# Partial sums loaded 42 products ahead, maxima turned before a run of products, stores listed two steps later

## The chip, the cores and the metric

The kernel runs on one core of a Trainium2 chip. The metric is the time of one execution on the device, in microseconds. Of several executions the median is given. The profile is one further execution, recorded by the hardware profiler; its own time is in the table below. In its lines PE is TensorE, DVE is VectorE, ACT is ScalarE, POOL is GpSimd and SP is SyncE, which here only issues transfers.

## What is computed

The input x has 2048 positions of 512 features. Two mixing layers run on it, and a gate for each position mixes their outputs:

```python
def _A_ref(x, dft_seq_re, dft_seq_im, dft_hid_re, dft_hid_im):
    a = jnp.einsum("bsd,ed->bse", x, dft_hid_re)
    b = jnp.einsum("bsd,ed->bse", x, dft_hid_im)
    return (jnp.einsum("ts,bse->bte", dft_seq_re, a)
            - jnp.einsum("ts,bse->bte", dft_seq_im, b))

def _B_ref(x, wqkv, wo):
    # 32 heads of 16 features; position i sees positions i-255 .. i
    ...
    scores = jnp.einsum("bhqd,bhkd->bhqk", q, k) * (Dh ** -0.5)
    p = _softmax(jnp.where(mask, scores, -1e9), axis=-1)
    o = jnp.einsum("bhqk,bhkd->bhqd", p, v)
    return o_as_rows @ wo

g = _sigmoid((x * gate_w).sum(-1, keepdims=True))
return g * _A_ref(...) + (1 - g) * _B_ref(...)
```

Everything is float32. The dense products are made from pairs of float32r tiles, a high part and a low part of each operand, as three products: high by high, high by low and low by high.

## The kernel before

**Two streams on one engine.** PE runs two streams of work, woven into one order written out by hand.

The *dense stream* is the generator `dense()`. It makes q, k and v, the DFT along the features (`ab_part`), and the DFT along the sequence, whose matrices come from HBM in pieces (`Pieces`: `load` brings a raw piece of 512 KB into one of two buffers, `split` makes its high and low parts with ACT at L141 and DVE at L142). Most of it runs in `halves64`: each step issues one product for partitions 0 to 63 (`first`) and one for partitions 64 to 127 (`second`, `DELAY` = 6 steps later). The unit is a `Part`, 12 or 24 products into one PSUM tile of 512 columns, and `second` takes the parts of a group in another order than `first`. An `Out` is the tile that one part, or several, add up in; when its last product has been issued, its `end` is called, which has the tile read out.

The sequence DFT is cut so that many outputs are finished in several rounds, since not all of its inputs fit into SBUF. `store_r` writes a first partial sum (ACT, L746) to a scratch tensor `r_scr` in HBM. A later round loads it again into an SBUF tile of the pool `ev` (five buffers that rotate), and `add_to` (DVE, L757) adds the new PSUM tile to it and stores the result. The load is `Out.load`, made by `fetch`; `product` calls it at L498, at the first product of the output's last half-part. There are 21 such outputs. After the attention `c_block` goes on with whole products (L547) and has its own load.

The *attention stream* runs over 128 blocks, n = 0 to 127: 8 groups of 4 heads by 16 blocks of 128 queries. Each iteration n has four quarters q. In the even ones `s_pair` makes scores of two heads (L338), and DVE masks them and takes their row extremes (L342). In the odd ones, nine iterations behind (`LAG`), `t_pair` makes the same scores transposed with the maxima subtracted (L397), ACT takes the exponential (L400), and POOL cuts the window's edges (L402, L406). Each takes one of two PSUM tiles of the pool `ps_a` in turn; a tile is free again when DVE, or ACT, has read it. `pv` multiplies by v (L420) every fourth iteration.

Every four iterations the maxima go from columns to rows: `ml_split` (DVE, L350 and L351) makes high and low parts, `ml_turn` (PE, L358) transposes them into a tile of `ps_a`, `ml_rows` (ACT, L363) copies them out, `m_out` and `m_ring` bring them through HBM into `ring`, where `t_pair` reads them nine iterations later.

**What sets the order.** The engines work in the order in which the program lists their instructions. In each quarter the loop at L1090 lists `s_pair` or `t_pair`, then what `agenda` holds for time 4n+q, then `fill`, which lists three or four steps of the dense stream (six to eight products), then what `agenda` holds for 4n+q+0.5. So an agenda time that ends in .5 comes behind the run of dense products and a whole one ahead of it. `after(n, fn)` lists a call n steps of the dense stream later. All loads and stores but a few go through SP (`ld`, L65), in the order listed; SP stops at one that has to wait.

**Names that matter here.** `STORE` (8) is the number of steps between the read-out of a PSUM tile into an `ev` tile and the listing of its store: for v (L307), first sums (L747), later sums (L758) and the outputs of `c_block` (L816). `ring_next` (L1024) lists the four loads of a group's next q and k into `ring`, at t+0.5, t+1.5, t+2.5 and t+3.5; t is set at L1080. The offsets of the maxima's steps are at L1066, counted from the third quarter of the last of four iterations.

Of the kernel before, what the change touches and what calls it, by code (L numbers as in the profile page):

```python
# [21 lines left out]
NB = S // P  # L22
# [7 lines left out]
DELAY = 6  # L30
# [4 lines left out]
RING_LATE = 5  # L35
JOB = 4
FIRST_OUT, PAIR = 104, 38
STORE, STORE_HL = 8, 11
FILL_T = 0.75


# [1 line left out]
def fnet_window_mix(ctx: ExitStack, tc: tile.TileContext, xT, x, wqk, wv, wr, wi, cr, ci, wo, gw, out):  # L43
# [84 lines left out]
    def beat():  # L128
        beats[0] += 1
        flush(beats[0])  # L130
# [14 lines left out]
    def job(n):  # L145
        if n % JOB == 0 and jobs:
            jobs.pop(0)()
# [341 lines left out]
    def product(part, half, i):  # L489
        o = part.out  # L490
        if o.ps is None:
            o.ps = ps_d.tile([P, 512], F32, name="d", tag="d")
            start = True
        else:
            start = False
        if part.ops is None:
            part.ops = part.make()
        if i == 0 and o.load and o.left == 1:  # L498
            o.r = o.load()
        lhs, rhs = part.ops[i]  # L500
        end = i == len(part.ops) - 1
        o.left -= end
        r = slice(64 * half, 64 * half + 64)
        nc.tensor.matmul(o.ps, lhs[r], rhs[r], start=start, stop=end and o.left == 0, skip_group_check=True)  # L504
        if end:
            if o.left:
                nc.scalar.copy(tick, o.ps[:, 0:1])
            else:
                o.end(o)

    def halves64(groups):
        first = [(p, i) for g in groups for p in g for i in range(p.n)]
        second = [(p, i) for g in groups for p in [g[-1], *g[:-1]] for i in range(p.n)]
        steps.append(len(first) + DELAY)
        for t in range(len(first) + DELAY):
            taken[0] += 1
            if t < len(first):
                part, i = first[t]
                if i == 0 and part.pre:
                    part.pre()  # L520
                if i in part.mid:
                    part.mid[i]()
                product(part, 0, i)
            if t >= DELAY:
                part_b, i_b = second[t - DELAY]
                product(part_b, 1, i_b)
            if t < len(first):
                job(i + 1)
            beat()
            yield  # L530
# [71 lines left out]
    def dense():  # L602
# [203 lines left out]

        c_groups[0][0].mid[12] = to_c
        yield from halves64(groups + c_groups)
        have.add("halves")

# [241 lines left out]
    def at_time(t, fn, *args):  # L1052
        agenda.setdefault(t, []).append((fn, args))
# [9 lines left out]
        at_time(4 * n + 8, v_spread, i)  # L1063
    for u in range(N // 4):
        t = 4 * (4 * u + 3) + 3
        for d, fn in ((0, ml_split), (2.5, ml_turn), (3, ml_rows), (3, m_out), (8, m_ring)):  # L1066
            at_time(t + d, fn, u)
    for i in range(4 * GROUPS):
        t = 4 * (VISIT * i + VISIT + LAG) + 3
# [7 lines left out]
    at_time(4 * (N + LAG - 12), wo_fetch, 0)  # L1077
    for G in range(1, GROUPS):
        for ss in range(4):
            t = 4 * (NB * G + 4 * ss) - 11.5  # L1080
            at_time(t, ring_next, t, G, ss)

    def run(t):
# [66 lines left out]
```

## Time and profile before

| | |
|---|---|
| median of 3 runs | 873.34 us (871.14 to 874.76) |
| profiled execution, its time | 869.23 us |
| profiled execution, its span | 867.5 us |
| granted TensorE clock, mean | 0.984 |
| DVE busy | 524.8 us (60%) |
| ACT busy | 409.4 us (47%) |
| data moved | 179.29 MB, mean 207 GB/s |

The span runs from the first instruction to the last; the time of the execution holds some 1.7 us more around it. Busy time counts an engine's instructions, and of the transfers the share of 16 DMA engines. A line such as "A <- B: 12.2, 5, 4.7" says that A's engine sat idle for 12.2 us in total, 5 times, at most 4.7 us, and that B ended it. In the timeline the columns are start, duration, engine, line, operation, what it writes and reads, and in brackets the idle time before it. "PEld" is the loading of weights, which lies beside the products.

### The profile page before, as it was taken

The numbers are of one execution on the slowest core, as the hardware profiler recorded it, in microseconds if no ns is written. First come the engines' busy times: TensorE is split into PE (matmuls) and PEld (weight loads), VectorE is DVE, ScalarE is ACT, GpSimd is POOL, SyncE is SP. The second block draws the span as 40 slices with busy tenths as digits, with TensorE's granted clock in tenths as the row PEclk, the third lists the DMA queues.
The fourth block names the chain that finished last, engine by engine and source line by source line (L and its number), as shares of the span: only waits on it lengthen the run. The fifth ranks groups of instructions, "written<-read, shape, count | busy, mean of one in ns | idle before, by whom it ended". The sixth has DMA issues, their size and how long they took to land.

```text
span 867.5 us, 19719 instructions
## 1 busy us (share of the span) xinstructions
PE 829.7 (96%) x7298; PEld 659.4 (76%) x7298; DVE 524.8 (60%) x1504; ACT 409.4 (47%) x794; POOL 315.4 (36%) x590
## 2 busy tenths in 40 slices
PE   8999999999989999999999999879889999899998
PEld 7898777777677777787778777657666778788887
DVE  6376676667566776666467666546556527455442
ACT  6235554556445555555555654335335655231320
POOL 4002333344233333333333343223223445574530
PEclk9999999999999999999999999989999999999999
DMA  8786787787968455545555657777886567765631
GB/s 310 248 257 188 255 263 231 233 259 255 299 231 282 127 169 177 169 142 159 178 159 170 182 183 199 228 222 215 243 255 210 172 194 224 229 217 168 209 109 49
DMA packets 111648, 179.29 MB, mean 207 GB/s; under 512 B 34240, under 2 KB 43968, under 8 KB 111552
## 3 DMA queue, kind: packets, MB, share of 16 engines
q1 hardware_dynamic: 109584, 176.85, 65.1%
q10 hardware_dynamic: 1968, 1.18, 0.5%
q8 instruction: 57, 0.93, 0.5%
q14 instruction: 39, 0.32, 0.1%
HBM read 112.98 MB, written 64.75 MB: 205 GB/s over the span
## 4 chain that ended last, share of the span: by engine, by line
PE 74%; DMA 14%; DVE 6%; issue 2%; SPq 2%; ACT 2%; POOL 1%; DVEq 0%; ACTq 0%; POOLq 0%
PE d L504 40%; PE o L420 8%; PE dc L547 8%; PE s L338 5%; PE t L975 5%; DMA raw<-ci 4%; PE t L397 4%; DVE junk L342 3%; PE d L534 3%; DMA qk_scr<-home 2%; SPq L65 2%; DMA raw<-cr 1%; DMA lt<-ots 1%; DMA ev<-l_scr 1%; DMA ring<-qk_scr 1%
## 5 line engine op out<-in xcount | busy, mean ns | idle before, releaser
L342 DVE CUSTOM_DVE_ANT_0 junk<-s,mask 128x384 f32<-128x384 f32 (+2 forms) x512 | 272.2, 532 | 199.2 <-PE s L338 188.6
L504 PE MATMUL d<-big,hi 64*128 64x512 f32 x1920 | 348.1, 398 | 0.0
L402 POOL TENSOR_SCALAR_AFFINE_SELECT pt<-pt 128x256 f32<-128x256 f32 x256 | 114.6, 447 | 458.8 <-ACT pt L400 357.6
L400 ACT ACTIVATE pt<-t 128x768 f32<-128x768 f32 (+2 forms) x256 | 197.7, 772 | 136.6 <-PE t L397 129.9
L504 PEld LDWEIGHTS d<-big,hi 64*128 64x128 f32 x1920 | 197.7, 189 | 27.3 <-issue 0.6
L504 PE MATMUL d<-big,lo 64*128 64x512 f32 x960 | 207.7, 399 | 0.0
L504 PE MATMUL d<-hi,big 64*128 64x512 f32 x672 | 132.1, 392 | 0.0
L338 PE MATMUL s<-ring,ring 48*128 48x384 f32 (+2 forms) x512 | 98.8, 358 | 20.3 <-DVE ml L342 14.6
L504 PEld LDWEIGHTS d<-big,lo 64*128 64x128 f32 x960 | 101.1, 189 | 13.7 <-issue 0.4
L141 ACT CAST hi<-raw 128x512 fp32r<-128x512 f32 x142 | 87.2, 618 | 35.5 <-DMA raw<-ci 17.3
L397 PE MATMUL t<-ring,ring 50*128 50x384 f32 (+2 forms) x512 | 88.7, 334 | 5.2 <-ACT mhl L363 4.1
L547 PE MATMUL dc<-big,hi 128*128 128x512 f32 x284 | 92.2, 394 | 0.0
L406 POOL TENSOR_SCALAR_AFFINE_SELECT pt<-pt 128x256 f32<-128x256 f32 x224 | 91.4, 408 | 0.0
L142 DVE TENSOR_TENSOR lo<-raw,hi 128x512 fp32r<-128x512 f32 x110 | 82.5, 750 | 13.8 <-ACT hi L141 13.7
L338 PEld LDWEIGHTS s<-ring,ring 48*128 48x128 f32 x512 | 53.6, 186 | 43.6 <-DVE ml L342 20.2
L420 PE MATMUL o<-pt,vt 128*32 128x384 f32 (+2 forms) x1408 | 85.3, 390 | 0.1
L504 PEld LDWEIGHTS d<-hi,big 64*128 64x128 f32 x672 | 75.6, 186 | 7.8
L504 PE MATMUL d<-lo,big 64*128 64x512 f32 x336 | 79.5, 392 | 0.0
L420 PEld LDWEIGHTS o<-pt,vt 128*32 128x32 f32 x1408 | 41.9, 111 | 47.5 <-issue 30.6
L397 PEld LDWEIGHTS t<-ring,ring 50*128 50x128 f32 x512 | 50.7, 187 | 19.7 <-ACT mhl L363 5.6
L547 PEld LDWEIGHTS dc<-big,hi 128*128 128x128 f32 x284 | 52.1, 189 | 8.6 <-DVE mask L871 0.2
L142 POOL TENSOR_TENSOR lo<-raw,hi 128x512 fp32r<-128x512 f32 x32 | 42.5, 1339 | 38.7 <-ACT hi L141 34.6
(113 smaller groups left out, 790.2 us busy)
## 6 DMA issues: line engine op xcount, KB each, us to landing
ring<-qk_scr SPq DMA_DIRECT2D x128, 192.0 KB
qk_scr<-home SPq DMA_DIRECT2D x32, 512.0 KB
raw<-cr SPq DMA_DIRECT2D x32, 512.0 KB
raw<-ci SPq DMA_DIRECT2D x32, 512.0 KB
r_scr<-ev SPq DMA_DIRECT2D x44, 256.0 KB
ab_scr<-home SPq DMA_DIRECT2D x20, 512.0 KB
big<-ab_scr SPq DMA_DIRECT2D x20, 512.0 KB
qk_scr<-home SPq DMA_DIRECT2D x32, 256.0 KB
```

The lines of the kernel that those rows point to most:

```text
L141: jobs.append(lambda c=c: nc.scalar.copy(hi[:, c], raw[:, c]))
L142: jobs.append(lambda c=c: (nc.gpsimd if FIN else nc.vector).tensor_sub(lo[:, c], raw[:, c], f(hi[:, c])))
L338: nc.tensor.matmul(ps[:, h, :w], ring[0][r, p, j * P:j * P + P], ring[1][r, p, k0:k0 + w], start=True, stop=True)
L342: mark("dve", nc.vector.tensor_tensor_reduce(out=junk[:, :w], in0=ps[:, h, :w], in1=mask[:, WIN - w:], scale=1.0, scalar=3e38, op0=OP.add, ...
L397: nc.tensor.matmul(ps[:, h, :w], ring[1][r, p, q0:q0 + P], ring[0][r, p, q0:q0 + w], start=True, stop=True)
L400: nc.scalar.activation(pt[:, ph, :w], ps[:, :, :w], AF.Exp, scale=-1.0)
L402: nc.gpsimd.affine_select(a, a, pattern=[[0, 2], [1, P]], compare_op=OP.is_ge, fill=0.0, base=0, channel_multiplier=-1)
L406: nc.gpsimd.affine_select(a, a, pattern=[[0, 2], [-1, P]], compare_op=OP.is_gt, fill=0.0, base=0, channel_multiplier=1)
L420: nc.tensor.matmul(o[32 * j:32 * j + 32, (a - 4 * c) * P:(e - 4 * c) * P], v[:, kb % 4, 32 * j:32 * j + 32], PT[G * NB + kb][:, j, (a - kb ...
L504: nc.tensor.matmul(o.ps, lhs[r], rhs[r], start=start, stop=end and o.left == 0, skip_group_check=True)
L547: nc.tensor.matmul(ps, w[a][:, i % 8 * 128:i % 8 * 128 + 128], ab[SC[i]][:, b], start=i == ends[0] and a + b == 0, stop=i == ends[1] and a ...
L975: nc.tensor.matmul(ps, o[:, a, c], fin(n, b, c), start=start and c == 0 and a + b == 0, stop=c == 1 and a == 1, skip_group_check=True)
```

## The change

Four numbers or places are changed.

- The load of a partial sum is no longer called in `product`. `halves64` works out for each output that has a load the step of its last product, in either half, and calls the load at the step `FETCH` = 42 before it.
- `STORE` is 10, not 8.
- `ml_turn` has the offset 2, not 2.5: it is listed right behind `t_pair` of the second quarter, ahead of that quarter's dense products, where it was behind them and right ahead of the next `s_pair`.
- The times of `ring_next` start 11 quarters ahead, not 11.5, so that its loads are listed behind a quarter's dense products, not ahead of them.

```diff
-STORE, STORE_HL = 8, 11
+STORE, STORE_HL = 10, 11
+FETCH = 42
...
-        if i == 0 and o.load and o.left == 1:
-            o.r = o.load()
...
+        ends = {}
+        for d, order in ((0, first), (DELAY, second)):
+            for t, (part, _) in enumerate(order):
+                if part.out.load:
+                    ends[part.out] = max(t + d, ends.get(part.out, 0))
+        fetches = {}
+        for o, t in ends.items():
+            fetches.setdefault(t - FETCH, []).append(o)
         for t in range(len(first) + DELAY):
             taken[0] += 1
+            for o in fetches.get(t, ()):
+                o.r = o.load()
...
-        for d, fn in ((0, ml_split), (2.5, ml_turn), (3, ml_rows), (3, m_out), (8, m_ring)):
+        for d, fn in ((0, ml_split), (2, ml_turn), (3, ml_rows), (3, m_out), (8, m_ring)):
...
-            t = 4 * (NB * G + 4 * ss) - 11.5
+            t = 4 * (NB * G + 4 * ss) - 11
```

## The prediction

> **What bounds the kernel now.** I read the page first, then the busy time by stretches.
>
> ```profile
> span 867.5 us, 19719 instructions
> ...
> PE 829.7 (96%) x7298; PEld 659.4 (76%) x7298; DVE 524.8 (60%) x1504; ACT 409.4 (47%) x794; POOL 315.4 (36%) x590
> ```
>
> TensorE (PE) is the bound. The view by windows (stretch, its length, busy time with instructions of PE, PEld, DVE, ACT, POOL, then granted clock, DMA share, GB/s) says where it isn't:
>
> ```profile
> 531.00:534.00 3.00, 3.00 (x32) 2.49 (x30) 2.74 (x8) 2.06 (x3) 0.76 (x2) 1.00 0.66 181
> 567.00:570.00 3.00, 3.00 (x30) 2.40 (x28) 1.28 (x5) 1.98 (x4) 0.85 (x3) 1.00 1.06 287
> 530.00:690.00 160.00, 141.87 (x1332) 107.33 (x1334) 95.20 (x280) 69.84 (x127) 50.30 (x111) 0.95 0.73 221
> 350.00:400.00 50.00, 50.00 (x520) 39.58 (x519) 32.31 (x99) 27.10 (x53) 19.33 (x41) 1.00 0.55 160
> ```
>
> From 350 to 400 us PE has no idle time: whatever makes it wait there adds to the total. From 530 to 690 it idles 18.1 us, with a clock of 0.95. The waits inside that stretch (us in total, times, longest):
>
> ```profile
> PE s L338 <- DVE ml L342: 12.2, 5, 4.7
> ...
> DVE ev L757 <- issue: 7.7, 2, 4.6
> ...
> DVE ev L757 <- DMA ev<-r_scr: 6.3, 2, 4.7
> ...
> DVE ev L757 <- PE t L397: 5.7, 2, 3.8
> ...
> ACT hi L141 <- DMA raw<-ci: 3.3, 2, 2.3
> ...
> PE t L397 <- ACT mhl L363: 1.6, 1, 1.6
> ```
>
> L757 is the add of a partial sum. It sat idle 19.7 us in these six waits. The timeline shows one of them whole:
>
> ```profile
> 562.45 0.58 SPq L65 DMA_DIRECT2D ev<-r_scr  x1
> ...
> 564.26 0.79 SPq L65 DMA_DIRECT2D raw<-ci  x1
> ...
> 573.02 0.75 DVE L757 SCALAR_TENSOR_TENSOR ev<-d,g,ev 128x512 f32<-128x512 f32 x1 [4.70 <-DMA ev<-r_scr]
> ...
> 575.50 0.69 PE L338 MATMUL s<-ring,ring 48*128 48x384 f32 x2 [4.72 <-DVE ml L342]
> ```
>
> The load is issued at 562.45 and its data is there at about 573.0: 10.5 us. DVE works in order, so the add blocks the mask-and-reduce of scores (L342) behind it; the score buffer stays occupied, and PE stops 4.72 us. The cost goes on after PE restarts:
>
> ```profile
> 546.00:552.00 6.00, 3.06 (x20) 2.25 (x18) 4.09 (x11) 1.62 (x3) 1.66 (x3) 0.82 0.56 177
> 552.00:558.00 6.00, 6.00 (x74) 3.72 (x72) 1.47 (x5) 1.99 (x4) 0.77 (x2) 0.90 0.51 149
> ...
> 570.00:576.00 6.00, 1.28 (x12) 0.81 (x10) 2.95 (x7) 0.88 (x2) 2.17 (x4) 0.81 0.64 183
> 576.00:582.00 6.00, 6.00 (x50) 3.30 (x48) 1.18 (x5) 0.97 (x2) 0.77 (x2) 0.62 0.54 159
> ...
> 618.00:624.00 6.00, 3.67 (x26) 2.37 (x26) 4.70 (x12) 1.58 (x3) 2.88 (x5) 0.79 0.75 190
> 624.00:630.00 6.00, 6.00 (x74) 3.95 (x71) 1.60 (x5) 1.97 (x4) 0.76 (x3) 0.93 0.58 189
> ...
> 642.00:648.00 6.00, 5.66 (x40) 4.50 (x44) 4.75 (x13) 1.69 (x3) 2.05 (x3) 0.72 0.69 221
> ```
>
> The granted clock falls behind each of the long stops. The shortfalls add up to 1.41, times 6 us 8.5 us; 0.9 of it falls while PE stands still at 573 to 575.5, so 7.6 us of slow work.
>
> **The loads (FETCH): -16.8.** The dense stream:
>
> ```profile
> L504 PE MATMUL d<-big,lo x960: 383/392/628, 34.1 to 716.7; 64*128 64x512 f32 x192
> ```
>
> It has 1950 steps (the counts of the four L504 groups, 1920, 960, 672 and 336, at two products a step, and 6 of delay) in 683 us: 0.35 us each. Today a load is issued at the first product of its output's last half, 23 steps or 8 us ahead of the last product; the add follows two steps later. The change makes it 42 steps, 14.7 us. The 10.5 us seen above then fit. No load is added, and 21 are moved 19 steps (6.6 us) up SP's queue, past raw pieces, reloads of the spectrum (big<-ab_scr), ring loads and the traffic of the softmax sums. It removes the 12.2 us of idle PE and, as the clock drops only behind stops, the 7.6 us of slow work: 19.8.
>
> What it gives back: the bytes stay. 0.73 of 160 us is 117 us of DMA work, and 160 less 20 us leaves a share of 0.84, in bursts that already reach 1.06 (the row of 567 to 570). The raw pieces of the DFT matrices stand behind the moved loads and already make ACT wait (3.3 us). Bounds: below nothing, -2, since the loads move into time with a share of 0.66 (the row of 531 to 534) and the raw pieces may land earlier for it; above, 13 of the 19.8, if the pieces arrive as late as the sums do now. I take 3, near the 3.3 us that the raw waits show.
>
> [...]
>
> **The turn (2.5 to 2): +12.** Every four iterations PE turns the row maxima (L358), in the score buffer that the scores just ahead of it used, so it waits until DVE has reduced those. Today six to eight dense products stand between; now the turn comes first and the products queue behind it, and then the next scores, ACT's copy of the maxima (L363) and DVE's next reductions. The first and the last turn that I could measure:
>
> ```profile
> 80.60 0.34 PE L338 MATMUL s<-ring,ring 48*128 48x384 f32 x2
> ...
> 81.69 0.34 PE L397 MATMUL t<-ring,ring 50*128 50x384 f32 x2
> ...
> 81.87 0.40 PE L504 MATMUL d<-big,hi 64*128 64x512 f32 x1
> ...
> 82.09 0.08 DVE L342 DVE_READ_ACCUMULATOR2_ANT ml<- 128x1 f32 x1
> ...
> 82.81 0.20 PE L358 MATMUL s<-ident,mlh 64*128 64x64 f32 x2
> ...
> 661.47 0.77 PE L504 MATMUL d<-big,hi 64*128 64x512 f32 x4
> ...
> 663.48 0.08 DVE L342 DVE_READ_ACCUMULATOR2_ANT ml<- 128x1 f32 x1
> 663.61 0.30 PE L358 MATMUL s<-ident,mlh 64*128 64x64 f32 x2 [0.91 <-DVE ml L342]
> ```
>
> At 82 us PE is free for the turn at 81.87 (where the dense product starts now); DVE is done at 82.17, and a waiting turn starts some 0.06 later (from 663.56 to 663.61). The new wait is 0.36 us. At 663 us the turn waits already and would wait longer by the products that no longer cover it, eight at 0.117, or 0.93. So for 29 turns: 4 wait nothing, 8 the whole run of products (6.8 us together), 17 on average 0.46 (7.8): 14.6. Two early turns without a measured neighbour get 0.35 each, the last none: 15.3. Against it, scores right behind a turn wait for the exponential today:
>
> ```profile
> PE s L338 <- DMA ring<-qk_scr: 3.2, 2, 2.5
> ...
> PE s L338 <- ACT pt L400: 2.0, 8, 0.4
> ```
>
> Five of the eight lie behind turns that will wait, 1.2 us. The six turns inside 530 to 690 make up 4.2; I count half of it as hidden in the transfers' waits already given back, since a later PE waits less for them: 2.1. That leaves 12.0. Bounds: 8 (17 at the smallest wait of 0.25 and half of the others), 15.3.
>
> **Stores and ring: 0.** SP's own waits:
>
> ```profile
> SPq L65 <- PE t L397: 29.4, 15, 6.6
> ...
> SPq L65 <- ACT ev L746: 20.1, 9, 4.8
> ...
> SPq L65 <- DMA o_scr<-ev: 13.8, 12, 2.4
> ```
>
> A store two steps later gives SP less to wait for (20.1 us on L746 alone) and holds a buffer 0.7 us longer; a ring load listed behind a run of products, not in front, is 0.9 us later in a queue that mostly waits for PE there anyway (29.4 us, 15 times). What covers both is that SP is not the bound: bounds -1 and, if both late ring loads of the row before come 0.9 us later, +2.
>
> **Sum.** -19.8 + 3 + 12.0 = -4.8. Against the profiled execution, 869.23 us (span 867.5 and 1.7 around it): 864.4. The median of the runs shown is 873.34, 4.1 above it; carried to that, 868.5 us.
>
> **The rivals.**
>
> *The turn costs little.* DVE may get ahead while PE waits, so that later turns find it done, and short stops elsewhere shrink. For it: DVE is busy 60% of the span, so it has time to catch up. Against it: from the scores' start to the end of their reduction 1.57 us pass at the first turn (80.60 to 82.17), and the turn's new place is only 1.27 us behind (81.87). At a third of the 12, or 4, the sum is -12.8: 860.5 us. Chance 0.18.
>
> *The wait moves to the raw pieces (slower).* Between 530 and 690 us PE then runs faster than DMA delivers; ACT waits for a piece, the exponential and the copy of the maxima behind it come late, and PE stops in L397 rather than L338, as in the row of 1.6 us. If 13 of the 19.8 come back, the sum is 13 - 19.8 + 12.0 = +5.2: 878.5 us. It is slower than before from a give-back of 7.8 on, which is a DMA share near 0.9 over the shortened stretch. For it: bursts at 1.06. Against it: 0.73 on average. Chance 0.20.
>
> *The loads don't move.* The five `ev` buffers rotate among sums, stores and softmax factors; SP already waits 13.8 us in the row for stores from them. A load that must wait for its buffer is issued no earlier, and holds the queue. Then the gain is small, say 6 of 19.8, with the turn's 12.0: +6.0, 879.3 us. Chance 0.07.
>
> [...] Chance 0.07.
>
> **How the numbers follow.** My forecast has 0.43, the rivals 0.18, 0.20, 0.07 and 0.07, anything else 0.05. About 0.5%, 4.4 us, is what a measurement of this kernel can tell from no change. The forecast itself lies just past it, so 0.27 of its 0.43 counts as faster and 0.16 as no change; the first rival adds 0.18 to faster; of the raw pieces' 0.20, 0.12 is slower and 0.08 no change; the loads that don't move are slower, the clock no change, the rest split. Faster 0.47, same 0.32, slower 0.21. Range: the terms' ends reach from -19.8 - 2 + 8 - 1 = -14.8 to 13 - 19.8 + 15.3 + 2 = +10.5; leaving out a tenth on each side, 859 to 879 us. The forecast's own part of it is 865 to 873.
>
> **What would show it.** Right, the loads: no wait of L757 above 1 us before 690 us, PE's waits on L342 inside 530 to 690 well under 12.2, clock near 1.00 there. Right, the turn: the turn's group L358 shows idle time of some 14 us where it had 3.6, in about 25 pieces, all along the kernel, with PE under 50.00 busy between 350 and 400. Right, the give-back: more idle time of ACT's L141 for raw pieces, or of L397 for L363. Wrong: L757 waiting as before (buffers), or the turn finding DVE done.

## The result, and the profile after

| | before | after |
|---|---|---|
| median of 15 runs each | 871.14 us (868.13 to 874.76) | 879.53 us (876.43 to 883.90) |
| ratio, 95% interval | | 1.0088 [1.0070, 1.0106] |
| profiled execution | 869.23 us | 876.43 us |
| granted TensorE clock, mean | 0.984 | 0.986 |

The change makes the kernel slower by 0.88%, 7.7 us. I had forecast 4.8 us less. The measured time lies 0.5 us past the upper end of the range.

The page of the changed kernel begins:

```profile
span 874.7 us, 19739 instructions
...
PE 831.6 (95%) x7298; PEld 654.4 (75%) x7298; DVE 520.5 (60%) x1504; ACT 407.7 (47%) x794; POOL 320.6 (37%) x590
```

PE is idle for 874.7 - 831.6 = 43.1 us, where it was 867.5 - 829.7 = 37.8: 5.3 us more. It is busy for 1.9 us longer. What ended PE's idle time shows that these 5.3 us are the difference of two large movements. First the view of PE's waits over the whole span of the kernel before (us in total, times, longest), without the rows that the prediction shows:

```profile
PE s L338 <- DVE ml L342: 14.6, 11, 4.7
PE t L397 <- ACT mhl L363: 4.1, 3, 1.7
PE s L358 <- DVE ml L342: 3.6, 6, 1.2
...
PE t L397 <- ACT pt L400: 0.7, 1, 0.7
```

The same view of the kernel after. Added code shifts the lines: L338 is L339, L358 is L359, L397 is L398, the add L757 is L766, and the cast of a raw piece, L141, is L142.

```profile
PE s L359 <- DVE ml L343: 11.5, 20, 1.6
PE s L339 <- DMA ring<-qk_scr: 9.7, 6, 4.5
PE t L984 <- ACT ex L127: 4.4, 1, 4.4
PE t L398 <- ACT pt L401: 3.9, 2, 3.3
PE s L339 <- DVE ml L343: 2.0, 6, 0.5
```

The stops behind the late adds are gone: scores wait for DVE 2.0 us instead of 14.6. In their place scores wait for their own q and k from the ring (9.7 instead of 3.2) and for the exponential (3.9 in L398 instead of 0.7). And the turn waits 11.5 us in 20 pieces, where it was 3.6 in 6.

The two stretches that the prediction singled out, in the view by windows (columns as there):

```profile
350.00:400.00 50.00, 48.72 (x488) 37.49 (x490) 33.13 (x106) 27.32 (x54) 19.50 (x41) 1.00 0.53 157
530.00:690.00 160.00, 145.61 (x1376) 111.86 (x1378) 96.24 (x294) 72.73 (x134) 52.96 (x115) 0.96 0.76 231
```

Between 350 and 400 us, where PE had no idle time, it now has 1.28 us, nearly all of it at the turn. Between 530 and 690 it idles 14.4 us instead of 18.1, at a clock of 0.96 instead of 0.95. The loads were to remove nearly all of it.

Did the loads come early enough? The view of the add's line says yes. Before, L757:

```profile
  DMA ev<-r_scr: 12.9, 4
  issue: 7.7, 2
  PE t L397: 5.7, 2
  PE d L504: 5.5, 6
```

After, the whole list of what ended DVE's idle time ahead of L766:

```profile
  PE d L503: 5.2, 6
  issue: 1.2, 3
  POOL pt L403: 1.2, 1
```

No add waits for its data any longer. So the change does what it says, and the loss needs two explanations: what the turn costs, and why the removal of 12 us of stops brought nothing.

The next table places it. It gives the start of the scores of block 32, 64 and 104, of the first product of `c_block`, and the end of the span, each read from the timelines as the distance to the kernel before, in us. Of the loads alone, the profiled execution lies 4.3 us under that kernel's median.

| | block 32 | block 64 | block 104 | `c_block` | end |
|---|---|---|---|---|---|
| kernel before, at | 179.9 | 344.8 | 537.8 | 717.1 | 867.5 |
| kernel after | +1.5 | +6.9 | +10.0 | +5.0 | +7.2 |
| turn alone | +2.1 | +3.9 | +7.0 | +8.9 | +7.3 |
| loads alone | +0.2 | -0.7 | -0.4 | -4.0 | -3.3 |
| before, 8.4 MB of loads left out | +0.1 | +1.3 | +1.0 | -19.8 | -19.2 |

The turn collects its loss over the whole length of the kernel. The last row, an experiment below, shows that some 20 us were to be had between block 104 and `c_block`, just where the prediction had looked. The changed kernel also loses 2.2 us behind the start of `c_block`. The row of L984 above has as much (4.4 us, where L975, the same line before, waited 2.2), but no experiment explains it.

### The profile page after: what moved, and what is told of

It reads as the page before. It is cut to its first block, busy times and chain, and to the rows that moved or that the text cites. A ratio compares the mean times of both kernels' runs of the same rounds, so it can differ in the third digit from the quotient of the medians.

```text
span 874.7 us, 19739 instructions
## 1 busy us (share of the span) xinstructions
PE 831.6 (95%) x7298; PEld 654.4 (75%) x7298; DVE 520.5 (60%) x1504; ACT 407.7 (47%) x794; POOL 320.6 (37%) x590
## 4 chain that ended last, share of the span: by engine, by line
PE 69%; DMA 18%; DVE 8%; issue 3%; ACT 1%; SPq 1%; POOL 1%; DVEq 0%; ACTq 0%; POOLq 0%
PE d L503 36%; PE dc L556 8%; PE o L421 8%; DMA ring<-qk_scr 6%; PE s L339 5%; PE t L984 5%; DVE junk L343 4%; PE t L398 3%; PE d L543 2%; DMA qk_scr<-home 2%; DMA raw<-ci 2%; DMA ev<-l_scr 2%; DMA o_scr<-ev 2%; DMA big<-ab_scr 1%; DMA raw<-cr 1%
## 5 line engine op out<-in xcount | busy, mean ns | idle before, releaser
L403 POOL TENSOR_SCALAR_AFFINE_SELECT pt<-pt 128x256 f32<-128x256 f32 x256 | 117.0, 457 | 462.1 <-ACT pt L401 355.6
L503 PEld LDWEIGHTS d<-big,hi 64*128 64x128 f32 x1920 | 194.6, 188 | 27.2 <-issue 0.6
L339 PE MATMUL s<-ring,ring 48*128 48x384 f32 (+2 forms) x512 | 97.7, 349 | 14.2 <-DMA ring<-qk_scr 9.7
L142 ACT CAST hi<-raw 128x512 fp32r<-128x512 f32 x142 | 87.1, 618 | 41.1 <-DMA raw<-ci 20.0
L398 PE MATMUL t<-ring,ring 50*128 50x384 f32 (+2 forms) x512 | 88.0, 333 | 6.0 <-ACT pt L401 3.9
L407 POOL TENSOR_SCALAR_AFFINE_SELECT pt<-pt 128x256 f32<-128x256 f32 x224 | 91.4, 408 | 0.0
L143 DVE TENSOR_TENSOR lo<-raw,hi 128x512 fp32r<-128x512 f32 x110 | 80.3, 730 | 17.3 <-ACT hi L142 11.3
L339 PEld LDWEIGHTS s<-ring,ring 48*128 48x128 f32 x512 | 53.5, 186 | 39.4 <-DMA ring<-qk_scr 9.9
L398 PEld LDWEIGHTS t<-ring,ring 50*128 50x128 f32 x512 | 50.5, 186 | 21.4 <-ACT pt L401 5.9
```

The costliest lines, as they stand in the source:

```text
L142: jobs.append(lambda c=c: nc.scalar.copy(hi[:, c], raw[:, c]))
L143: jobs.append(lambda c=c: (nc.gpsimd if FIN else nc.vector).tensor_sub(lo[:, c], raw[:, c], f(hi[:, c])))
L339: nc.tensor.matmul(ps[:, h, :w], ring[0][r, p, j * P:j * P + P], ring[1][r, p, k0:k0 + w], start=True, stop=True)
L398: nc.tensor.matmul(ps[:, h, :w], ring[1][r, p, q0:q0 + P], ring[0][r, p, q0:q0 + w], start=True, stop=True)
L403: nc.gpsimd.affine_select(a, a, pattern=[[0, 2], [1, P]], compare_op=OP.is_ge, fill=0.0, base=0, channel_multiplier=-1)
L407: nc.gpsimd.affine_select(a, a, pattern=[[0, 2], [-1, P]], compare_op=OP.is_gt, fill=0.0, base=0, channel_multiplier=1)
```

## The experiments

Each ratio is to the kernel before on the same chip, with its 95% interval; 0.1% is 0.87 us.

### One part at a time: the turn

```diff
-        for d, fn in ((0, ml_split), (2.5, ml_turn), (3, ml_rows), (3, m_out), (8, m_ring)):
+        for d, fn in ((0, ml_split), (2, ml_turn), (3, ml_rows), (3, m_out), (8, m_ring)):
```

> Only the turn moves (offset 2 in the kernel before). Theory A (the turn costs PE waits, as in the prediction: +12.0 in all, and the trace of after is 10.0 us late at block 104, before the first load that was moved): 881 to 884 us against 871, PE idle before the turn's products 10 to 14 us against 3.6. Theory B (the turn costs little and the lateness before block 104 comes from the later stores or ring loads): within 3 us of before.

Measured: 877.61 us, 1.0084 [1.0055, 1.0112], or 7.3 us (4.8 to 9.8). That is less than the 881 to 884 us expected, and still nearly the whole loss of the change. The page, then PE's waits:

```profile
span 874.8 us, 19726 instructions
...
PE 832.1 (95%) x7298; PEld 650.9 (74%) x7298; DVE 525.4 (60%) x1504; ACT 410.0 (47%) x794; POOL 316.4 (36%) x590
```

```profile
PE s L358 <- DVE ml L342: 14.9, 24, 2.0
PE s L338 <- DVE ml L342: 11.3, 9, 2.9
...
PE t L397 <- ACT mhl L363: 2.2, 2, 1.6
...
PE s L338 <- ACT pt L400: 0.3, 2, 0.2
```

The turn's own wait grew by 14.9 - 3.6 = 11.3 us, in 24 pieces. But PE's whole idle time is 874.8 - 832.1 = 42.7 us, only 4.9 above that of before: other waits shrank by a net 6.4 us, scores behind DVE by 3.3, the copy of the maxima by 1.9, the exponential by 1.7. A stop at the turn would let the other engines catch up, so that the next wait is shorter; the two profiles fit this, but no run shows it by itself. With 2.4 us more of busy time this is the span's 7.3.

### The turn undone in the changed kernel

```diff
-        for d, fn in ((0, ml_split), (2, ml_turn), (3, ml_rows), (3, m_out), (8, m_ring)):
+        for d, fn in ((0, ml_split), (2.5, ml_turn), (3, ml_rows), (3, m_out), (8, m_ring)):
```

> The kernel after with the turn at 2.5 again. Theory A: 10 to 12 us faster than after, so 867 to 870 us, 2 to 4 us faster than before. Theory B: no faster than after.

Measured: 872.34 us, 1.0033 [1.0011, 1.0055]. By the ratios (1.0088 and 1.0033) that is 4.8 us less than the changed kernel, where 10 to 12 were expected, and the turn's 7.3 us alone lie within what the two intervals leave open. What is left, loads, stores and ring together, is no gain: it loses 2.9 us (1.0 to 4.8), where a gain of 2 to 4 was expected.

### Every second turn

```diff
-            at_time(t + d, fn, u)
+            at_time(t + (2 if fn is ml_turn and u % 2 else d), fn, u)
```

> The kernel before with every second turn (16 of 32) at offset 2. Theory A (each moved turn adds its own wait of PE): half of the 8.2 us that all of them cost, 3 to 5.5 us slower than before. If only a few turns carry the cost: under 2 or over 6.5 us.

Measured: 873.20 us, 1.0029 [1.0012, 1.0045], or 2.5 us (1.0 to 3.9). The point lies below what was expected, the interval reaches into it. The loss grows with the number of turns moved. In proportion, half of the 7.3 us would be 3.7, which the interval holds; more can't be said of it.

### One part at a time: the loads

```diff
-STORE, STORE_HL = 10, 11
+STORE, STORE_HL = 8, 11
...
-(2, ml_turn)
+(2.5, ml_turn)
...
-            t = 4 * (NB * G + 4 * ss) - 11
+            t = 4 * (NB * G + 4 * ss) - 11.5
```

(against the changed kernel, so that `FETCH` alone is left)

> Only the loads move (FETCH 42; stores, turn and ring as before). Theory A (the loads' stops go, and a part comes back as waits for ring loads behind the moved loads): 5 to 10 us faster than before, no wait of the add of a partial sum over 1 us up to 690 us, ring loads late by several us in all. The prediction's own term: 16.8 us faster. Theory C (the ring's offset, not the moved loads, makes the ring loads late): some 15 us faster and no late ring loads.

Measured: 870.30 us, 1.0004 [0.9970, 1.0038]: 0.3 us more (2.6 less to 3.3 more). The largest term of the prediction, -16.8, isn't there, and neither are the 5 to 10 us that were expected of this run. The page and PE's waits of this kernel:

```profile
span 864.2 us, 19721 instructions
...
PE 826.9 (96%) x7298; PEld 659.1 (76%) x7298; DVE 526.4 (61%) x1504; ACT 409.4 (47%) x794; POOL 316.1 (37%) x590
```

```profile
PE s L339 <- DMA ring<-qk_scr: 8.5, 4, 5.2
PE t L398 <- ACT pt L401: 6.5, 3, 3.7
...
PE s L339 <- DVE ml L343: 2.5, 6, 0.9
```

Scores waiting for DVE lost 14.6 - 2.5 = 12.1 us, as predicted (12.2). The ring took 8.5 - 3.2 = 5.3 of it, the exponential 6.5 - 0.7 = 5.8, 11.1 together. PE's idle time is 37.3 us, as good as the 37.8 of before. The clock between 530 and 690 us is 0.97 in this run, where it was 0.95.

One place shows the exchange. Before, in the timeline:

```profile
547.67 0.75 DVE L757 SCALAR_TENSOR_TENSOR ev<-d,g,ev 128x512 f32<-128x512 f32 x1 [4.63 <-issue]
...
549.55 0.51 PE L338 MATMUL s<-ring,ring 48*128 48x384 f32 x2 [2.94 <-DVE ml L342]
```

With the earlier loads, at the same place:

```profile
537.20 0.38 SPq L66 DMA_DIRECT2D raw<-cr  x1
...
544.09 0.75 DVE L766 SCALAR_TENSOR_TENSOR ev<-d,g,ev 128x512 f32<-128x512 f32 x1
...
547.76 0.62 ACT L142 CAST hi<-raw 128x512 fp32r<-128x512 f32 x1 [5.44 <-DMA raw<-cr]
...
549.14 0.45 PE L398 MATMUL t<-ring,ring 50*128 50x384 f32 x2 [3.75 <-ACT pt L401]
```

The add now runs 3.6 us earlier, without a wait. But the raw piece issued at 537.20 is there only at 547.76, 10.6 us later; ACT's cast of it holds the exponential, and PE restarts at 549.14 instead of 549.55. (Before, the same piece was issued at 536.99 and its cast began at 546.74.) The first of these windows, of the kernel with the earlier loads, has the time in which that piece is under way:

```profile
540.00:546.00 6.00, 5.37 (x48) 4.18 (x48) 4.38 (x12) 0.94 (x3) 1.79 (x3) 1.00 1.02 326
564.00:570.00 6.00, 6.00 (x55) 4.91 (x53) 4.77 (x16) 3.98 (x8) 1.59 (x4) 1.00 1.01 296
```

The DMA engines are full in both, with a share of 1.02 at 326 GB/s and 1.01 at 296. Behind the second window comes the longest of the new waits for the ring. It has another immediate cause. Here are the load that PE waits for and the end of the wait, with the earlier loads:

```profile
581.37 1.17 SPq L66 DMA_DIRECT2D ring<-qk_scr  x1
...
589.64 0.47 PE L339 MATMUL s<-ring,ring 48*128 48x128 f32 x1 [5.21 <-DMA ring<-qk_scr]
```

The same load before, which nothing waited for, since PE came to these scores only at 590.41:

```profile
581.48 0.71 SPq L65 DMA_DIRECT2D ring<-qk_scr  x1
```

From issue to use it takes 8.3 us. That isn't long: between 350 and 450 us, in the kernel before, the 21 ring loads took 7.0 us in the median and 8.2 at most from issue to landing, read from the landing events in the trace. So this load is hardly slow under way, it is issued late. Between 566 and 582 us SP waits 10.5 us, in seven pieces, for transfers issued earlier to land, the sums' moved loads among them:

```profile
SPq L66 <- DMA ev<-r_scr: 2.5, 2, 1.3
```

The transfers of the full window land late, and SP, which issues in order, stands still behind them. So the ring load leaves no earlier than before (0.1 us), while PE, no longer stopped by the add, comes for it 6.0 us earlier.

### Fewer bytes, and more

```diff
         def next_b():
             sc = todo_b.pop(0)
-            nxt[sc] = load_ab(1, sc)
+            nxt[sc] = ab[sc]
```

> The kernel before without the 16 reloads of the spectrum's imaginary part (8.4 MB; the products take the real part's tiles instead). Theory D (the sums, the raw pieces and the ring loads are late together, because a burst of transfers is longer than the time that their lead gives): with the burst a quarter smaller the stops between 530 and 690 us shrink though the loads are listed as before, 12 to 20 us faster than before, DVE's waits for sums under 5 us against 19.7. Theory E (the sums are late because they are listed late): the waits for sums stay over 12 us, under 6 us faster.

Measured: 849.17 us, 0.9749 [0.9709, 0.9788], or 21.8 us less. The time is what theory D expected and a little more. The sums' own waits for DMA between 525 and 690 us, expected under 5 us by D and over 12 by E, were 8.1, so not everything followed the expectation:

```profile
DVE ev L757 <- DMA ev<-r_scr: 8.1, 4, 3.1
```

The windows of before, and of this kernel, from 525 to 690 us:

```profile
525.00:690.00 165.00, 146.87 (x1402) 110.41 (x1400) 97.12 (x285) 71.62 (x132) 52.57 (x116) 0.95 0.73 219
```

```profile
525.00:690.00 165.00, 159.28 (x1610) 121.81 (x1610) 103.16 (x295) 85.36 (x154) 65.13 (x140) 1.00 0.67 192
```

PE's idle time falls from 18.1 to 5.7 us and the clock rises to 1.00. (The faster kernel has more work in the same 165 us, so the shares are of stretches and not of equal work.)

The loads moved early (`FETCH` 42 as above), on top of this:

> The same leaving out, with the loads 42 products ahead. Theory D: within 4 us of the run without reloads and with the old loads, since the burst and not the lead decides. Theory E: 10 us or more faster than that run.

Measured: 849.87 us, 0.9772 [0.9730, 0.9814]. Even with fewer bytes the earlier loads are worth nothing that can be seen.

This removal takes 16 issues out of SP's queue along with the bytes. So the opposite was tried with a transfer that nobody reads and that SP doesn't issue:

```diff
+    idle_scr = [dram.tile([P, 2, D], F32, name=f"idle_scr{c}") for c in range(16)]
...
+            mark("pool", nc.gpsimd.dma_start(idle_scr[sc], ab_scr[1][sc]))
```

(the second line in `next_b`, beside each reload)

> The kernel before with a copy of 512 KB from HBM to HBM beside each of the 16 reloads, issued from POOL's queue, read by nobody. Theory D (the transfer engines' time in the burst is the limit): 10 to 25 us slower than before, sums, raw pieces and ring loads later. Theory F (places and waits in SP's queue are the limit): within 4 us of before.

Measured: 882.17 us, 1.0180 [1.0133, 1.0226], or 15.7 us more. The queue's row on the page, and the same window:

```profile
q0 software_dynamic: 512, 8.39, 2.8%
```

```profile
525.00:690.00 165.00, 138.65 (x1270) 106.39 (x1268) 89.72 (x271) 64.16 (x120) 54.73 (x119) 0.91 0.82 257
```

8.39 MB more cost 15.7 us, about as many less brought 21.8. Over the stretch the DMA share goes 0.67, 0.73, 0.82, PE's idle time 5.7, 18.1, 26.4 us, the clock 1.00, 0.95, 0.91. So with the program's order as it is, more bytes in this stretch mean more stops, also when SP doesn't issue them. (What the issuing costs POOL isn't measured by itself; in the next run POOL issues 28 loads and the loss is 0.4%.)

### Is it SP's queue?

```diff
-                ld(r, src)
+                mark("pool", nc.gpsimd.dma_start(r, src))
```

(with `FETCH` 42 and the rest as before)

> The loads 42 products ahead, issued from POOL's queue instead of SP's (stores, turn and ring as before). Theory D1 (the transfer engines' throughput in the burst is the limit): within 4 us of the loads alone on SP (870.3 us, ratio 1.0004 to before). Theory D2 (SP's queue is the limit: it lets only about eight transfers be under way and issues in order): 8 us or more faster than before.

Measured: 871.89 us, 1.0040 [1.0013, 1.0067]. The trace of the kernel before has at most eight transfers under way when one is issued, that one counted (eight at 127 of its 732 issues, by the landing events); what keeps them to eight was not tried. The waits from 530 to 690 us:

```profile
PE s L339 <- DMA ring<-qk_scr: 8.8, 4, 4.6
...
ACT hi L142 <- DMA raw<-ci: 6.0, 2, 4.0
```

With the sums' loads taken out of SP's queue, the ring loads and raw pieces that were listed behind them are late all the same. So it isn't the places of the moved loads in SP's queue that make them late. SP itself isn't cleared by this: the wait of 4.6 us ends at 592.62 with a ring load that was issued at 584.26, 8.4 us ahead, after SP had again waited for raw pieces, reloads and others to land. Whether ring loads issued from another queue would be there in time was not tried.

### A smaller lead, and reloads spread out

A lead between the 23 steps of before and 42, the rest as before:

```diff
-FETCH = 42
+FETCH = 30
```

> The loads 30 products ahead, the rest as before. Theory D (the burst decides, whichever of the transfers is late): within 4 us of before and of the loads at 42. If a middle lead shared the lateness out so that none stops PE: 5 to 10 us faster than before.

Measured: 871.06 us, 1.0013 [0.9989, 1.0037]. No gain here either.

The reloads of the spectrum one per part over seven parts, in place of eight in five, first in the kernel before, then with `FETCH` 42:

```diff
-                if n in (1, 2, 3, 4, 5):
+                if n < 7:
                     mid[12] = next_b
-                if n in (1, 3, 5):
+                if n == 3:
                     mid[20] = next_b
```

> The kernel before with the eight spectrum reloads of a phase spread evenly over its seven parts (one in the middle of each, one more), not put into five of them. Theory D (the burst's length decides): 2 to 8 us faster than before by smaller peaks; nothing if the peaks come from the attention's transfers in step with the raw pieces.

> The same spread with the loads 42 products ahead. Theory D: again within 4 us of the run with the spread and the old loads.

Measured: 868.75 us, 0.9992 [0.9968, 1.0015], and 872.94 us, 1.0045 [1.0021, 1.0069]. The second is 4.6 us slower than the first, a little more than expected. That the bursts could be levelled so was not borne out; the spread covers only a small part of the traffic.

### Another pace of the dense stream

The dense stream's share per quarter was raised ahead of the crowded stretch and lowered in it, so that the stretch lasts longer for the same bytes; then more of the same, then with the loads moved, then the reverse.

```diff
-        share = [1.0 if m < N else FILL_T for m in range(n, N + LAG + 1)]
+        share = [1.0 if m < 56 else 1.08 if m < 98 else 0.88 if m < N else FILL_T for m in range(n, N + LAG + 1)]
```

> The kernel before with the same work in another mixture: 8% more dense steps per block in blocks 56 to 97, 12% fewer in 98 to 127, where the burst is. Theory D (the stops come from bytes asked for faster than they come): fewer late transfers behind block 98, 3 to 10 us faster than before. Theory F (the reloads' waits for buffers on SP's queue, not the bytes, made the lateness): within 2 us of before.

> The same with 16% more and 24% fewer. Theory D: faster than the milder mixture by a further 2 to 6 us, unless the tail behind the attention grows. Theory F: within 3 us of before.

> The milder mixture with the loads 42 products ahead. Theory D: within 4 us of the milder mixture with the old loads.

> The kernel before with 8% fewer dense steps per block in blocks 56 to 97 and 12% more in 98 to 127 (the pace runs turned round). Theory D (rate of bytes): the burst gets denser, 4 to 12 us slower than before, sums and raw pieces later. Theory G (the ring loads' lead is a number of quarters, so longer quarters give them more time): waits for ring loads near zero and 3 us or more faster than before.

Measured: 875.02 us, 1.0061 [1.0040, 1.0083] with 1.08 and 0.88; 890.66 us, 1.0228 [1.0190, 1.0267] with 1.16 and 0.76; 878.62 us, 1.0097 [1.0067, 1.0128] with `FETCH` 42 on the first; 876.30 us, 1.0073 [1.0042, 1.0104] with 0.92 and 1.12. PE's waits of the first and of the last:

```profile
PE s L338 <- DMA ring<-qk_scr: 17.3, 8, 3.7
```

```profile
PE s L338 <- DMA ring<-qk_scr: 11.9, 8, 3.7
```

Slower in both directions, with the ring's wait grown from 3.2 us each time. Theory D had the first faster by 3 to 10 us and the second faster still; they were 5.3 and 19.8 us slower, so against these two runs it fails. The window of the second (1.16 and 0.76):

```profile
525.00:690.00 165.00, 138.29 (x1242) 103.13 (x1240) 95.72 (x299) 68.21 (x123) 56.00 (x117) 0.92 0.73 209
```

PE idles 26.7 us there at fewer GB/s than before (209 against 219), as long as with the 8.39 MB more. So the mean rate of bytes alone doesn't set the stops. The pace decides how many products lie between a ring load's listing and its use as well as how fast the bytes are asked for, and these runs don't part the two. Why a thinner stretch didn't relieve the ring stays open.

### Stores and ring

```diff
-STORE, STORE_HL = 8, 11
+STORE, STORE_HL = 10, 11
```

> Only the stores move (10). The prediction: 0, between -1 and +2 us. If those 2 to 3 us come from the stores: +2 to +3 us.

```diff
-            t = 4 * (NB * G + 4 * ss) - 11.5
+            t = 4 * (NB * G + 4 * ss) - 11
```

> Only the ring's offset moves (11). The prediction: 0, between -1 and +2 us. If the 2 to 3 us by which the kernel with loads, stores and ring changed is slower than the one with the loads alone come from the ring: +2 to +3 us.

And this second edit undone in the changed kernel:

```diff
-            t = 4 * (NB * G + 4 * ss) - 11
+            t = 4 * (NB * G + 4 * ss) - 11.5
```

> The kernel after with the ring loads listed at 11.5 again. Theory A (the ring loads are late by the transfers ahead of them, of which half a quarter changes little): within 2 us of after. Theory C: the 8.1 us of waits for ring loads between 530 and 690 us go, 6 to 10 us faster than after.

Measured: stores 870.39 us, 1.0008 [0.9983, 1.0032]; ring 868.90 us, 0.9989 [0.9963, 1.0015]; ring undone 880.62 us, 1.0107 [1.0070, 1.0143], no less than the changed kernel's 1.0088. The ring's new 9.7 us of waits don't come from its changed place. No version that ran is shown to be faster than the kernel before with the same work.

## Why the prediction was wrong

**The loads, -19.8: right in what they remove.** All adds get their data in time, and 12.1 us of PE's waits on DVE went, where the prediction had 12.2. The prize was of the right size too, though it took fewer bytes to get it: with 8.4 MB less, the stretch gained 18.1 - 5.7 = 12.4 us of idle time and 0.05 x 165 = 8.3 us of clock, 20.7 us together.

**The give-back, 3: this step failed.** The sum with the loads alone came out at +0.3 us, so 20.1 us came back (17.2 to 23.1), all of the term and more than my upper bound of 13. The prediction read the delay of 10.5 us as that of a late issue, to be cured by an earlier one. But the load was under way while the DMA engines were full (a share of 1.01 between 564 and 570 us), and a raw piece in the same burst took 10.6 us as well. The ring loads are late by way of SP, which stands behind transfers that land late: the one of the longest wait left SP 0.1 us earlier than before, and PE came for it 6.0 us earlier. I had the share of 1.06 and the 0.84 of the shortened stretch, and took the mean for slack. But the bytes per iteration don't change, and a PE that stops less would only ask for them faster. The experiments with fewer and more bytes speak for this, and the one with POOL's queue against the moved loads' places in SP's queue. What stays open is how much of it is the DMA engines' speed and how much SP's waiting for earlier transfers, and why the slower pace didn't help. The rival of the raw pieces had the mechanism. It named one of the two places where the wait came back and missed the ring. Its threshold, a mean share near 0.9, was an estimate that it doesn't work out, and too high: stops are there at 0.73 already, and mostly gone at 0.67 with the bytes left out.

**The turn, +12.0: right in mechanism and sign, too large.** The runs give 7.3 us (4.8 to 9.8), just under my lower bound of 8. New waits at the turn were 11.3 us in 24 pieces, where the working had 15.3 in some 25; other waits gave back a net 6.4, where I had 3.3; and PE was busy 2.4 us longer, which I had not counted. The signs named beforehand appeared: L359 with 11.5 us in 20 pieces in the changed kernel, and 48.72 busy in 50 us. The rival of a cheap turn, at 4, lies below the interval of the turn alone, but the 4.8 us from the turn undone don't exclude it.

**Stores and ring, 0:** as predicted for each alone. Whether they cost something together with the loads (1.0033 with all three, 1.0004 with the loads, the intervals overlap) stays open.

**The rivals.** "The loads don't move" fell with the list of L766. That the clock would stay low for a cause other than the stops, at a chance of 0.07, fell with the run with fewer bytes: PE's idle time between 525 and 690 us went from 18.1 to 5.7 us, and the clock from 0.95 to 1.00.

**The sum.** -19.8 + 20.1 + 7.3 + 0 = +7.6, against the measured 7.7. With the give-back right and the turn as predicted the forecast would have been +12. So it was luck that the time came out only 0.5 us past the range: the turn, taken 4.7 us too high, made up for a part of the 17.1 us missing in the give-back.

## What to carry to other kernels

Before moving a late transfer forward, look at the DMA share in the microseconds in which it is under way: where it was 1.01 and 1.02 here, an earlier issue only chose who was late, so work out what else lands there, which engine waits behind it, and whether the queue that issues the next loads stands still for it. Price such a stretch by taking bytes out and by adding idle ones, which here answered with -22 and +16 us, while no other order or pace that was tried gave anything. A wait moved onto the busiest engine's own order can cost less than the sum of its new pieces; here 11.3 us of pieces made 7.3, with other waits shorter.

## What was not expected of the hardware

The clock after short stops. In the changed kernel the timeline has a stop at the turn of only 1.59 us, and the windows the clock behind it:

```profile
204.80 0.30 PE L359 MATMUL s<-ident,mlh 64*128 64x64 f32 x2 [1.59 <-DVE ml L343]
```

```profile
201.81:205.22 3.41, 1.81 (x14) 1.42 (x16) 2.86 (x8) 1.05 (x3) 1.94 (x4) 1.00 1.04 398
205.22:208.64 3.42, 3.42 (x20) 2.85 (x18) 1.29 (x5) 0.34 (x2) 0.00 (x0) 0.50 1.02 393
```

The clock is 0.50 for the 3.4 us behind the stop. In the kernel with fewer bytes a stop of nearly twice that length has a clock of 1.00 behind it:

```profile
569.57 0.45 PE L338 MATMUL s<-ring,ring 48*128 48x384 f32 x2 [2.98 <-DVE ml L342]
```

```profile
555.00:585.00 30.00, 27.00 (x258) 20.95 (x255) 20.50 (x64) 15.34 (x28) 10.63 (x26) 1.00 0.74 206
564.39:567.80 3.41, 2.20 (x20) 1.51 (x18) 0.71 (x2) 1.89 (x4) 2.75 (x5) 1.00 0.43 121
567.80:571.21 3.41, 1.64 (x16) 1.42 (x18) 3.34 (x11) 0.05 (x1) 0.00 (x0) 1.00 0.47 153
```

So of these two stops it was the shorter one that cost clock. The shorter lies within one of the windows, together with other pauses (PE busy for 1.81 us of 3.41); the longer is spread over two (2.20 and 1.64 us of 3.41). What decides, the two places don't show. What a stop costs in clock was read here from the windows behind it, and not from its length.
